# Three weight pieces issued by another engine, and a new order of all steps, in a DeltaNet and MLP kernel

## The chip, the core and the metric

One core of a Trainium2 chip runs the whole program. The metric is device time in microseconds (us), the median of several runs; lower is better. TensorE (PE; PEld are its weight loads) multiplies matrices into PSUM banks, VectorE (DVE), ScalarE (ACT) and GpSimd (POOL) work elementwise, and SyncE (SP) issues DMA transfers. ScalarE and GpSimd issue transfers too. Each engine works off its own list of instructions in order; an instruction that has to wait holds up all that stand behind it on its engine.

## The reference

```python
B, H, S, D = 4, 8, 768, 48
k_n = k / (norm(k) + 1e-6)
for t in range(S):                      # state: D x D for each batch and head
    y[t] = q[t] @ state
    v_old = k_n[t] @ state
    state += beta[t] * outer(k_n[t], v[t] - v_old)
x = y with heads joined                 # B x S x 384
xn = (x - mean) / sqrt(var + 1e-6) * g_ln
out = x + relu(xn @ w_ch1) @ w_ch2      # 384 -> 1536 -> 384
```

The activations are float32. The two weight matrices lie in memory as 64-bit numbers, and the kernel makes float32 of them.

## The kernel before

**Chunks.** The 768 time steps are cut into 12 chunks of 64. Within a chunk the recurrence is written as products: the Gram matrix of the keys, the inverse of a triangular 64x64 matrix for each of the 32 heads, and products with the state that the chunk before left. A head's work is a 64x64 product, so TensorE runs them in groups of 32 or 64 small products.

**The start-up.** Chunk 0 makes its inverse by doubling, in five levels (`first_inverse`). At each level TensorE makes a product with the Gram matrix (L785), VectorE copies the masked part of it (L790), TensorE multiplies the inverse so far by it (L803), and VectorE (L750) and ScalarE (L744) copy the result back for the next level. The bit masks for this are built by VectorE (L465, L471, L477) from two index tables of GpSimd (`xor` and `bits`, L435 and L436). Each level waits for the one before. Then come the queries of chunk 0 (product L837, multiplied by a mask by VectorE, L868), `u` (products L1087, VectorE L1092), the output `y` (L1113, ScalarE copy L1151), its layer norm (VectorE L1157 to L1169, ScalarE L1163), transposes of the normed rows (L1201) and their scaled copies by ScalarE (`xnt`, L1217). At the same time the keys of chunks 2 and 3 are transposed (L635).

Chunk 1's inverse starts from blocks of 16 rows, which VectorE inverts by substitution in a chain of 30 small steps (`rows_inverse`, called x0: L925 and L932). It gets its input from DRAM (`gb`) and writes its result to DRAM (`xd`), from where eight small transfers bring it into place (`xt`). Later pairs of chunks do the same with blocks of 32 rows (x1, x2, ...), and join the blocks by products (L999, L1005).

**The weights.** They come in twelve pieces of two halves, 384 KB each (`fetch`), into five word buffers, three of which are used again. A piece is turned into float32 by four steps (`convert`): ScalarE scales the high words (L599), VectorE shifts them (L604), ScalarE scales the low words (L607), and GpSimd adds both into the weights (L617). Pieces 0 to 5 are `w_ch1`, 6 to 11 `w_ch2`. Pieces 5, 6 and 7 (the sixth to the eighth) go into the buffers that pieces 2, 3 and 4 leave, so their transfers wait for the GpSimd sums of those.

**The MLP.** It follows each chunk (`mlp`). For chunk 0 the first layer is plain products of 128 columns (L1424) with a relu by ScalarE (L1432) and the second is L1466. Chunks 1 and 2 have a first layer in 256 columns (L1444). From chunk 3 on the first layer is made by a scheme of fifteen block products (L1325, with sums by VectorE L1348, ScalarE L1343 and GpSimd L1308), and from chunk 1 on the second layer is made by seven half-size block products (L1541, sums L1528, L1559, L1566). Results go out in `put`.

**The order.** Every piece of work is a step, added by `Line.add` with the engine that does it and the tiles that it reads and writes. The program is not emitted in the order in which the steps are made. A long text, `ORDER`, lists all 3032 step numbers; `Line.emit` walks along it, and `in_this_order` fixes each engine's list to that sequence:

```python
for w in ORDER.split():
    a, b = (0, -1) if w in "fF" else map(int, (w.split("-") * 2)[:2])
    order += self.steps[a : b + 1] or [w]
```

A number may stand anywhere behind the steps that it depends on. An `f` stands for a filler: a product of the identity matrix that nobody reads (`idle`, L1618). The old text has one, in the fifth level of chunk 0's inverse. Waits follow from the tiles alone, so where a step stands decides only what stands before and behind it on its own engine. For transfers that step is the issue: `dma` (L409) issues from the queue of the engine that is named.

Of the kernel before, what the change touches and what calls it, by code (L numbers as in the profile page):

```python
# [159 lines left out]
232 92 97 218 130-131 129 230 220 109 258 253 251 140 137 222 136 91 138 27 31 141 139 142 146 34 143 152 148 24 26 147 158 32 154  # L160
153 231 210 96 145 144 149-151 157 155-156 95 160 159 162 164 161 163 168 28-29 169-170 98 205 165 207 206 174 166 212 167 173 172
171 255 254 252 257 256 395 307 305 176 317 402 405 318 401 47 233 175 178 177 219 184 180 185-186 655 653 658 226 214 182-183 238
188 181 242 187 189 192 259 240 221 209 f 4 179 193 190 194 191 215 223 35 211 250 260-262 241 263 265 201 197 202 204 236 199 203
200 198 309 195 310 264 243 235 234 228 362 237 239 196 329-333 335 353 311 355 312 224 356 361 313-314 354 266-268 337 269-270
338 341 216 315 246 271-288 342-343 289-295 427 321-322 324 323 334 429 336 325-326 347 339-340 348-350 327 344 316 396 399 296
404 406 217 213 328 225 303 298 302 403 301 300 299 468 304 469 426 297 466-467 394 397 400 244 567 569 568 428 345-346 351 571
570 357 572 245 227 352 657 659 229 247 666 660 430 575 593 363 576 359 579-580 594 431 573 583 599 432 407 365 574 584 600 587
577-578 588 358 364 661 410 408 392 409 366 360 605 581 591 368 582 592 606 470 367 411 611 585-586 412 597 589-590 413 598 379
374 612 595-596 603 369 371 601 630 604 602 373 434 1068 668 465 471-474 476-482 414 483-485 667 415 370 372 670 1067 391 669 665
416 609 418 610 420 380 417 631-632 615-617 433 375 419 421-422 633-635 607 618 385 425 386 423-424 435-436 608 381 377 613  # L170
619-620 783 785 782 787 486-498 376 499-507 382 508-511 671-672 378 512 673 383 513 384 1080 916 786 789 788 779 784 918 614 437
440 442 445 441 387 438 443 439 636 621 637 662 638-639 514 444 446-447 450 389 663 674-675 515 388 516 390 1070 1072 677 517 448
790 451 518 449 452 519-539 622-623 457 640 453 641 624-626 1174 780 664 924 676 926 681 540 680 678-679 541 543 542 544 475 642
627 460 456 454 459 458 791 455 794 821-822 825 827 826 831-832 823 828 837 682 824 833 838 843 792 645-647 651 648-650 683-686
848 845 1082 781 1069 688 1071 1073 1084 846 1083 1074 847 1079 545 793 546 834 839 548 550 547 549 551 553 552 555 554 795
689-700 556 829 796 840 830 844 797 835 854 864 917 928 1173 927 925 930 929 923 931 1179 1181 849 922 463 701-705 800 802 798 855
805 706 806 799 1075 856-857 836 865 858 801 841 859 810 842 860 921 1180 643 1183 644 628 1184 629 1185 1365 1171 1178 1182
919-920 932 557 1086 852 862 850 464 851 861 853 866-868 811-812 871 817 1085 461-462 1542 1081 863 803 652 804 933 869 881 872
882 934 807 558 561 819 818 560 559 562 707-710 808-809 711 936 870 712-717 813 883-885 889 886 873-876 878-879 1544 877 887 1087
1554 880 814 816 815 566 564 563 820 565 935 937 972 896-901 890-894 938 973 1546 888 1556 1545 1555 1558 1541 1543 1091 1559  # L180
718-719 1186 978 939 941 720-725 1548 996 726-729 940 895 730 902 731-751 687 1076 979 943 1077 984 974-975 942 907-910 1088 1190
911-912 980 944 946-947 945 913 985 1089 951 981 948 990 976-977 986-987 991 982 1005-1007 983 988 1008-1010 989 994 992 1361 1368
1360 1370 1369 1078 1172 1372 1176 752 904 903 905 1090 997 906 756 753-755 1366 1177 952 949-950 953 955 969 954 1092 956 1093
1367 1371 757-758 1187 768 960 1175 1094 958 1373 1362 1095 957 1374 914-915 959 759 1011 964 999 1002 998 967 1000 968 1547 1003
1012 1022 993 1032 1023-1025 995 1015-1016 1033 1017 760 762 761 763 766 764 767 1188-1189 1549 1191 965-966 1013 1001 1004 1014
765 1018 1026-1027 1019 1034-1036 1020-1021 1192 1040-1041 1037 1042-1045 1375 1030 1557 970-971 1219 1223 1653 1655 1657 1659
1363 1652 1193 1196 769 1194 1842 1648 1654 1656 1658 1840 962 1096 963 1038-1039 1029 1238 1031 1028 1097-1098 1046 1099-1100
2030 1102 1234 1220-1221 773 772 1198 771 1058-1062 1239 1047-1048 1195 1201-1202 770 1197 1199-1200 1203-1204 1103 1560 1224 1376
774 776 775 1206 1049 1063 1050-1052 777 961 778 1227 1553 1377 1064 1207 1104 1053 1105 1205 1106-1110 1208 1111 1101 1112
1235-1236 1228-1229 1237 1230 1251 1231-1232 1252 1210 1233 1240-1241 1209 1253-1254 1378-1379 1246 1242 1247 1222 1243-1244 1270  # L190
1261 1055 1225 1262 1226 1380 1561 1245 2032 1054 1280 1248-1250 1258 1255-1256 1263-1264 1259 1257 1266-1267 1265 1113 1660 1114
1260 1271-1272 1268 1115-1116 1281-1282 1381 1647 1211 1650 1845 1056 1215 1364 1214 1847 1057 1839 1213 1846 1212 1646 1065 1848
1841 1838 1844 1066 2034 1275 1273 1117 1283 1118-1120 1274 1269 1284-1286 1382 1308 1276-1277 1309 1298-1299 1310 1383 1311 1292
1289-1291 1296 1287-1288 1312 1300 1313 1293 1295 1121-1123 1278 1124 1305 1301-1303 1325 1216 1304 1279 1306 1326 1315-1317
1217-1218 1294 1297 1307 1408 2035 1327 1318-1320 1328 1324 1322 2036 1323 1415 2042 1384 1125 1314 1333 1329-1330 1334-1338
1126-1132 1331 1340-1341 1409 1342-1345 1133-1135 1339 1419 2031 1332 1550 1410 1351 1423 1321 1412 1352 1413 1136-1138 1346 1411
1353-1355 1416 1356 1417 1385 1551 1562-1563 1418 2033 1427-1428 1139-1143 1414 1144-1145 1357 1146-1165 1429-1430 1424-1425 1420
1432-1433 1421 1387 1426 1439-1440 1661 1422 1431 1837 1552 1645 1849 1564 1166 1569 1851 1358 1568 1169-1170 1167-1168 1359
# [57 lines left out]
def kernel(  # L256
# [1514 lines left out]
```

## Time and profile before

| What | us |
|---|---|
| Three runs: lowest, median, highest | 513.07, 513.96, 515.15 |
| The profiled execution, its own time | 513.69 |
| Its span | 512.0 |
| TensorE busy | 481.8 (94%) |
| VectorE busy | 357.4 (70%) |
| GpSimd busy | 282.3 (55%) |
| ScalarE busy | 206.2 (40%) |
| TensorE's mean granted clock | 0.983 of full |
| First MLP product (L1424) starts | 60.5 |
| Weight transfers issued by ScalarE (24 of 384 KB) | 12.7 to 91.4 |

A line of the chain of waits says when a stretch of the chain that ended last began, how long it took, and what it was; "issue" is time in which an engine waited for nothing that the profile shows. "ACTq" and "SPq" are the instruction sequencers of ScalarE and SP, here issuing transfers. A line such as "PE by L785 x32" is 32 products of line 785 into the bank `by`.

### The profile page before, as it was taken

The numbers are of one execution on the slowest core, as the hardware profiler recorded it, in microseconds if no ns is written. First come the engines' busy times: TensorE is split into PE (matmuls) and PEld (weight loads), VectorE is DVE, ScalarE is ACT, GpSimd is POOL, SyncE is SP. The second block draws the span as 40 slices with busy tenths as digits, with TensorE's granted clock in tenths as the row PEclk, the third lists the DMA queues.
The fourth block names the chain that finished last, engine by engine and source line by source line (L and its number), as shares of the span: only waits on it lengthen the run. The fifth ranks groups of instructions, "written<-read, shape, count | busy, mean of one in ns | idle before, by whom it ended". The sixth has DMA issues, their size and how long they took to land.

```text
span 512.0 us, 22780 instructions
## 1 busy us (share of the span) xinstructions
PE 481.8 (94%) x9968; PEld 446.6 (87%) x9968; DVE 357.4 (70%) x814; ACT 206.2 (40%) x462; POOL 282.3 (55%) x447
## 2 busy tenths in 40 slices
PE   4677799999999999999999999999999999999997
PEld 3566697768898899899988999999999999999996
DVE  4847658897988667999868898688788436253241
ACT  4577744633443144323334522524513425324130
POOL 8024385224874996784465574634462831654554
PEclk9777999999999999999999999999999999999999
DMA  9986787559456855364644563734424601212011
GB/s 128 257 188 124 211 150 179 123 148 159 82 92 127 204 103 81 85 120 113 136 96 70 105 132 102 130 86 103 88 39 98 140 8 46 52 46 50 2 32 31
DMA packets 181635, 54.56 MB, mean 107 GB/s; under 512 B 164888, under 2 KB 177312, under 8 KB 181536
## 3 DMA queue, kind: packets, MB, share of 16 engines
q1 hardware_dynamic: 168512, 40.10, 38.9%
q10 hardware_dynamic: 10816, 9.83, 6.5%
q0 software_dynamic: 2208, 3.17, 4.0%
q8 instruction: 78, 1.28, 1.1%
q14 instruction: 21, 0.17, 0.1%
HBM read 36.30 MB, written 16.78 MB: 104 GB/s over the span
## 4 chain that ended last, share of the span: by engine, by line
PE 83%; DVE 6%; DMA 3%; issue 3%; SPq 3%; ACT 2%; ACTq 0%; DVEq 0%
PE f L1541 29%; PE f L1325 21%; PE f L1444 6%; PE two L837 3%; PE f L1424 3%; SPq L409 3%; PE by L1051 2%; PE two L1051 2%; PE f L1466 2%; PE two L1106 2%; PE two L1123 2%; PE by L1113 2%; DMA kr<-in_k_dram 2%; PE f L803 1%; PE by L785 1%
## 5 line engine op out<-in xcount | busy, mean ns | idle before, releaser
L1528 POOL TENSOR_TENSOR h_all<-h_all 128x256 f32<-128x256 f32 x99 | 73.5, 755 | 20.4 <-DVE tmp L925 8.4
L1541 PE MATMUL f<-w_sb,h_all 128*128 128x192 f32 x396 | 79.2, 330 | 0.0
L1541 PE MATMUL f<-words,h_all 128*128 128x192 f32 x396 | 77.3, 330 | 0.0
L1348 DVE TENSOR_TENSOR h_all<-f,h_all 128x512 f32<-128x512 f32 x72 | 49.0, 686 | 28.5 <-PE f L1325 21.8
L1541 PEld LDWEIGHTS f<-w_sb,h_all 128*128 128x128 f32 x396 | 65.0, 190 | 1.5 <-issue 0.2
L1541 PEld LDWEIGHTS f<-words,h_all 128*128 128x128 f32 x396 | 64.8, 190 | 0.8
L1566 POOL TENSOR_TENSOR words<-h_all 128x128 f32<-128x128 f32 x66 | 30.0, 472 | 54.0 <-ACT h_all L1352 28.5
L1343 ACT COPY h_all<-f 128x512 f32<-128x512 f32 x45 | 26.2, 585 | 81.3 <-PE f L1325 52.3
L932 DVE TENSOR_TENSOR xb<-xb,tmp 128x31 f32<-128x31 f32 (+19 forms) x139 | 53.6, 386 | 3.5
L925 DVE TENSOR_TENSOR tmp<-xb,gb 128x31 f32<-128x31 f32 (+19 forms) x139 | 51.7, 372 | 4.1 <-POOL xb L912 0.3
L1352 ACT ACTIVATE h_all<-h_all 128x512 f32<-128x512 f32 x54 | 32.5, 626 | 32.5 <-DVE h_all L1348 32.4
L409 POOL DMA_DIRECT2D tb<-in_k_dram x64 | 41.9, 657 | 0.9 <-issue 0.7
L1325 PE MATMUL f<-xnt,w_sb 128*128 128x128 f32 x288 | 39.6, 278 | 0.1
L1325 PE MATMUL f<-x_new,w_sb 128*128 128x128 f32 x288 | 39.5, 277 | 0.0
L1325 PEld LDWEIGHTS f<-x_new,w_sb 128*128 128x128 f32 x288 | 36.4, 192 | 0.3
L1325 PEld LDWEIGHTS f<-xnt,w_sb 128*128 128x128 f32 x288 | 36.0, 192 | 0.6 <-DVE h_all L1348 0.2
L1444 PE MATMUL f<-xnt,w_sb 128*128 128x256 f32 x144 | 33.8, 385 | 0.0
L1559 DVE TENSOR_TENSOR o<-f,x 128x192 f32<-128x192 f32 x33 | 11.3, 348 | 28.4 <-PE f L1541 18.3
L1444 PEld LDWEIGHTS f<-xnt,w_sb 128*128 128x128 f32 x144 | 26.7, 190 | 3.8 <-DVE o L1475 0.4
L1541 PE MATMUL f<-w_sb,words 128*128 128x192 f32 x132 | 26.4, 330 | 0.3 <-DVE o L1559 0.3
L617 POOL TENSOR_TENSOR w_sb<-words 128x768 uint32<-128x768 uint32 (+1 forms) x11 | 14.9, 1365 | 16.4 <-ACT words L607 14.7
L1541 PEld LDWEIGHTS f<-w_sb,words 128*128 128x128 f32 x132 | 21.5, 190 | 0.9 <-DVE o L1559 0.6
(237 smaller groups left out, 976.1 us busy)
## 6 DMA issues: line engine op xcount, KB each, us to landing
words<-in_moe_w_ch_dram ACTq DMA_DIRECT2D x20, 384.0 KB, 4.9
gd<-gsb SPq DMA_DIRECT2D x11, 512.0 KB, 3.7
v<-in_v_dram SPq DMA_DIRECT2D x24, 192.0 KB, 4.1
kr<-in_k_dram SPq DMA_DIRECT2D x46, 96.0 KB, 3.5
out_dram<-o SPq DMA_DIRECT2D x46, 96.0 KB, 2.4
xld<-xlt SPq DMA_DIRECT2D x9, 384.0 KB, 2.3
xnt<-xld SPq DMA_DIRECT2D x36, 96.0 KB, 2.9
tb<-in_q_dram SPq DMA_DIRECT2D x40, 64.0 KB, 3.7
```

The lines of the kernel that those rows point to most:

```text
L409: add(eng, cost, lambda: QUEUE[eng].dma_start(out=out_, in_=in_), r, w, bulk=n * ns / 16e3, np=n, **kw)
L925: lambda j=j, n=n, w=w, t=t: nc.vector.tensor_tensor(out=t, in0=xv[:, 0:n, j : j + 1].to_broadcast([128, n, w]), in1=gv[:, j : j + 1, j + ...
L932: "DVE", dve(n * w), lambda t=t, rest=rest: nc.vector.tensor_tensor(out=rest, in0=rest, in1=t, op=ALU.subtract),
L1051: nc.tensor.matmul(dst[half(e), hp, j], src[drows(hp), (e if n else key_half(c, hp, e)) * GP + j], s_all[drows(hp), e, j], start=(n == 0 o ...
L1325: nc.tensor.matmul(wide(p[:, f : f + 128]), w[:, f : f + 128], r, start=start and i == 0, stop=True, skip_group_check=True)
L1343: add("ACT", act(512), lambda: nc.scalar.copy(o, p), pk, ok)
L1348: add("DVE", dve(512), lambda: nc.vector.tensor_tensor(out=o, in0=x, in1=y, op=op), [*xk_, *yk], ok)
L1352: add("ACT", act(512), lambda: nc.scalar.activation(o, o, ACTF.Relu, scale=scale), [], ok)
L1444: nc.tensor.matmul(p[:, 0:TOK], w1_sb[:, t, f * 128 : (f + 1) * 128], xnt[:, t], start=(t == 0), stop=(t == KC - 1))
L1528: add(eng, cost, lambda: e.tensor_tensor(out=out_, in0=x, in1=y, op=op), r, w, port=2 if eng == "Pool" else 1, pr=-2)
L1541: lambda f=f, t=start and f == order[0]: nc.tensor.matmul(p[:, 0:D2], lhs(f), rhs[:, f], start=t, stop=(f == order[-1]), skip_group_check=True
L1566: lambda f=f + i: e.tensor_tensor(out=s3[f], in0=one(0, 0)[0](f), in1=one(1, 0)[0](f), op=ALU.subtract),
```

## The change

The diff has two parts. In `fetch`, the six transfers of the sixth to the eighth piece are issued by SP in place of ScalarE:

```diff
         for a in range(2):
             dma(
-                "ACT", dst[:, a], src[:, a].rearrange("p (b x) -> p b x", x=2 * RUN), 384, 54,
+                "SP" if 5 <= i < 8 else "ACT", dst[:, a], src[:, a].rearrange("p (b x) -> p b x", x=2 * RUN), 384, 54,
                 w=[("wd", BUF[i], a)], after=after, **kw,
             )
```

The other part is a new text `ORDER`, 96 lines in place of 95, of which the first three are shown:

```diff
 ORDER = """
-51-52 54 58 53 55 57 319 56 63 62 306 398 67 308 393 66 320 7 65 64 9 8 59 61 60 249 11 10 48 12 49 654 656 50 248 68 0 3 2 13
-71-72 46 40 44-45 42-43 41 101-102 1 75 36 82-84 76-77 73-74 37 103 38 104 99 93 39 94 100 90 85-86 78 15 14 69 208 87 89 105-108
-16-18 79-80 70 81 110 88 111 114-118 121 119 113 120 124 112 122 25 19-20 125 123 132 126 134 6 5 22 133 30 128 127 33 21 23 135
+52 54 0 2 53 58 51 57 56 55 319 63 66 306 394 308 62 67 320 64 249 7-8 48 9 65 60 10 49 59 11-12 14 16 21-22 18 6 13 3 72 71 42 61
+654 656 248 68 101-102 40 46 43 50 44 41 45 1 75 82 76 83 73 77 84 36 74 104 103 37-38 100 99 93 39 94 105-106 34 24 33 19 78
+85-86 79 69 23 107 89 87 80 20 15 70 88 81 17 116-117 110 118 111-112 122 90 121 120 113 108 119 124-125 132 123 31 208 114-115
...
```

The steps are the same in number and kind, but for the filler, which is gone. What each engine's list becomes, by the place of each step in it (the six moved transfers left out):

| Engine | Steps | In the same place | Within three places | Over ten places off | Farthest |
|---|---|---|---|---|---|
| TensorE | 954 | 201 | 646 | 32 | 25 |
| VectorE | 814 | 152 | 596 | 64 | 89 |
| ScalarE | 483 | 103 | 385 | 9 | 41 |
| GpSimd | 443 | 66 | 315 | 32 | 70 |
| SP | 332 | 40 | 171 | 65 | 65 |

On SP the moved transfers stand as follows among the first steps of its list: the sixth piece's first half behind the loads of chunk 3's keys, then the seventh's second half, a `beta_b` load, the second half of chunk 1's queries, the sixth's second half, a load for chunk 1's norms, the seventh's first half, four more small loads, the write of chunk 2's Gram matrix, the eighth's second half, a `beta_b` load, the write of x0's result, and the eighth's first half. At the end of chunk 0's inverse TensorE's list was: level-5 product (one half of the heads), filler, level-5 product (the other half), half of the queries, both last products of the inverse, transposes of chunk 2's keys, the other half of the queries. It is now: both level-5 products, one of the last products, both halves of the queries, `u` for half of the heads, the other last product.

More of the change, by code (lines that the diff above doesn't have):

```diff
@@ L161 @@
[L161 to L188, printed above, removed]
@@ L252 @@
+2957-2958 2897-2898 2888-2889 2961 2959 2926 2960 2970-2971 2980-2981 2972-2973 2982-2985 2974-2975 2986 2964 2962-2963 2967 2977
+2968 3005-3006 2976 2965-2966 2969 2978 2987 2950 2997-2998 3007-3008 2988 2979 2951 3009 2999-3002 2989 3010 3003 3012-3013 2990
+3014 2991-2992 3015-3017 3011 3018 2993-2996 3004 3023-3028 3019-3020 3029 3021 3030 3022 3031
 """
```

154 lines of the change are left out of this document (90 added, 64 removed).

## The prediction

> **What bounds the kernel now.** I read the 40 slices first, then the busy times of three long stretches, then the chain of waits of the first 70 us, then the clock.
>
> ```profile
> PE   4677799999999999999999999999999999999997
> ...
> PEclk9777999999999999999999999999999999999999
> DMA  9986787559456855364644563734424601212011
> ```
>
> TensorE is under 80% busy in the first five slices (64 us) and full from there to the last one. The clock is below full in slices 2 to 4, and the DMA engines are busiest in the first eight.
>
> ```profile
> 0.00:63.00 63.00, 40.67 (x1231) 35.11 (x1232) 39.85 (x130) 41.59 (x97) 24.79 (x43) 0.86 0.84 178
> 63.00:504.00 441.00, 436.91 (x8716) 407.77 (x8716) 316.25 (x681) 164.61 (x366) 255.73 (x402) 1.00 0.46 97
> 504.00:512.00 8.00, 4.20 (x25) 3.67 (x23) 1.34 (x4) 0.00 (x0) 1.74 (x3) 0.96 0.18 49
> ```
>
> Columns: stretch, its length, busy us of PE, PEld, DVE, ACT, POOL, granted clock, DMA share, GB/s. TensorE idles 63 - 40.67 = 22.3 us before 63 us and 441 - 436.91 = 4.1 us in the 441 us after it. The matrix work is the same in both kernels but for one filler product, so the change can gain a few us in the start-up, at most 4 in the long stretch, and can lose in both.
>
> ```profile
> 39.98 1.13 PE by L785 x32
> 41.11 0.72 PE two L1618 x2
> 41.84 1.30 PE two L785 x32
> 43.14 0.76 PE by L837 x27
> 43.90 0.98 PE f L803 x51
> ...
> 45.31 0.37 ACTq L409
> ...
> 45.73 0.50 ACTq L409
> ...
> 46.91 0.65 PE f L635 x4
> ...
> 50.79 0.84 issue
> ...
> 56.75 1.10 issue
> ```
>
> This is the chain (start, us, what) where chunk 0's inverse ends. The reader should see a filler on it (L1618), two weight issues of ScalarE (ACTq L409) between copies that TensorE waits for, and TensorE standing for "issue" in the middle of groups of products, while DMA is heavy.
>
> **The change, part by part.** All times are those of the profiled execution. T is the start of VectorE's mask multiply of chunk 0's queries (L868), at 46.82; the MLP's first product (L1424) starts at 60.53, 13.7 us after T.
>
> *Before T, at the inverse's end.* From 39.98 to T the old TensorE order is: level-5 product 1.13, filler 0.72, level-5 product 1.30, half of the queries 0.76, both last products of the inverse (L803) 0.98, transposes of chunk 2's keys (L635) 0.65, the other half of the queries 0.50 + 0.32 wait + 0.46; with hops, 6.84. In the new one the filler is gone (-0.72), one of the two L803 groups (half of 0.98, -0.5) and the key transposes (-0.65) stand behind the second half of the queries. Sum -1.87. The second level-5 product has its input: its VectorE copy ended at 40.51, so the filler's time is free to be saved. Bounds: 0 (something else ends last) and -2.2 (its 0.32 wait goes too).
>
> *Before T, in VectorE's queue.* Mask building that stands between dependent steps at 18.61 (0.26 and 0.30) and 21.88 (two memsets of 0.27) moves to the front, where VectorE idles from 3.18 to 6.31 waiting for GpSimd's `bits`; GpSimd now makes `bits` ahead of two of its DMA issues (0.65 and 0.80). One mask step of 0.2 comes in between instead: -0.9. Against it, ScalarE's two square roots of the key norms (9.03 and 9.49) now stand behind the copy of the first keys, some 0.4 later, while chunk 1's keys are issued one place (0.65) sooner. I take 0 for these two together, bounds -0.7 and +0.7.
>
> *The moved issues.* Six issues of 0.55 leave ScalarE (3.3 us of its queue between 45.31 and 51.78; 0.87 is on the chain above). On SP each needs its word buffer free: the sixth piece's first half goes at about 38, but the seventh's waits for GpSimd's sum of the fourth piece (L617, 48.22 to 49.68 now, some 2 us sooner in the new order), and SP stands there. Behind it: one `beta_b` load, half of chunk 1's queries, the sixth piece's second half, the norm loads, the write of chunk 2's Gram matrix. Chunk 1's queries would land at about 52, their transposes stand at 54.98 and 59.79 now: hidden, by 3 us or more. The eighth piece's last half to go stands behind the write of x0's result (L409 xd, which waits for the L925/L932 chain, over at 57.81).
>
> *From T to the first MLP product.* VectorE in the new order: mask multiply 1.22, first `u` 0.56, one weight shift (L604) 0.56, the L925/L932 chain with the layer norm's steps 8.41 (49.40 to 57.81), second `u` 0.55: 11.3. Then either shift 0.42 and GpSimd's weight sum 0.82, or transposes of the normed rows 0.55 and three scaled copies 0.89: 12.5 to 12.9 against 13.7. I take -0.8; bounds 0 and -1.2. So the first MLP product comes 1.87 + 0.9 + 0.8 = 3.6 us sooner, near 57.
>
> *What is late next.* The fifth feature block needs the sum of a second weight half (L617); counted the same way it is ready at T + 17.4, and the old order uses it at 64.58, T + 17.8: of the 0.8 only 0.4 stays (+0.4). The eighth piece's last half is issued at about T + 12 and lands 4.9 later (median of its group), T + 16.9; ScalarE wants it at T + 15.5, with the MLP's relus queued behind. Three banks of products cover most of that 1.4: +0.3, bounds 0 and +1.4.
>
> *The long stretch.* Of 954 TensorE steps 646 stay within three places, the largest move is 25. Loads of `k` by GpSimd move up to 25 places and SP's up to 41 in the first 150 us. Counting TensorE work between each load and its user in both orders, 62 users stand short of the median landing in the old order and 59 in the new. I take 0; bounds -2 (half of the 4.1 us idle) and +4 (twice that idle).
>
> Sum: -3.6 + 0.4 + 0.3 = -2.9. The profiled execution took 513.69 (span 512.0, 1.7 around it), 0.27 under the median of the runs, 513.96. Taken from the median: 511.1.
>
> **The clock.**
>
> ```profile
> 19.78:26.60 6.82, 5.91 (x160) 5.30 (x164) 4.59 (x18) 4.34 (x10) 0.00 (x0) 0.50 0.91 293
> 26.60:33.43 6.83, 4.31 (x181) 3.61 (x178) 4.01 (x14) 5.02 (x16) 0.00 (x0) 1.00 0.90 235
> 33.43:40.26 6.83, 4.78 (x153) 4.21 (x147) 3.69 (x11) 4.92 (x12) 5.33 (x7) 0.50 0.88 117
> 40.26:43.67 3.41, 3.41 (x97) 3.00 (x97) 1.19 (x4) 2.88 (x7) 0.22 (x1) 0.50 0.48 59
> ```
>
> The granted clock goes back to full after stretches with 5.91 of 6.82 and 3.41 of 3.41 us busy, and to half after one with 4.31 of 6.83. The removed filler lies in the last of these, and gives 0.72 of its 3.41. Without it the next product follows at once, so I forecast the same clock. The Trainium skill (TensorE: Matmul & The Clock Gate, "HAM oscillation — how this bites in real kernels") has the half clock come back after an idle gap of more than about 3.4 us. This trace differs: it fell to half after a stretch whose longest stand is 1.38 us. By the page a missing filler could not matter; by the trace it could.
>
> **The rivals.**
>
> *Given back.* The start-up shortens, but waits for weights and loads behind SP's stand take its place in the first MLP block. For it: SP stands some 9 us, and TensorE already waits for L617 at 60.53 (0.34). Against it: the 3 us of cover. The gain falls to about 0.5: 513.4.
>
> *Half clock.* One mechanism: the stretches near 27 and 41 us fall under what the gate wants, and the start-up runs at half until the MLP. A 32-product group (L785) takes 0.69 at full (18.07) and 1.13 at half (39.98), 1.64 times. The chain has 3.1 us of TensorE work from 26.6 to 33.4 and 10.2 from 43.7 to 60; 13.3 x 0.64 = 8.5 if all counts, and I take 5.5, since VectorE's 11.3 us chain covers part. 513.96 - 2.9 + 5.5 = 516.6. It decides from the point where the extra passes 2.9 us, that is 4.5 us of chain work at half. For it: two of five stretches were that thin. Against it: a shorter chain is a denser one.
>
> *Waits in the long stretch.* The new places cost TensorE four or five further waits of about 1 us, like the 1.1 of the chain at 56.75, over eleven chunks: 511.1 + 4 = 515.1 and up. For it: 308 TensorE steps moved by over three places. Against it: the count of short users is no larger.
>
> *Stalls go too.* The "issue" stands of 1.38, 1.00, 0.84 and 1.10 us (29.72, 35.77, 50.79, 56.75) all fall where transfers are dense; with transfers spread out, three of the four (3.3) go: 507.8. For it: none as long stands elsewhere before 200 us. Against it: pieces one to five stay where they were.
>
> *Not what it says.* The pieces go when their buffers come free, as now; then only ScalarE's 0.87 is saved. That would be 513.1, and is counted with the second case.
>
> **How the numbers follow.** Shorter start-up, kept: 0.48, own range 509.2 to 512.9. Given back: 0.16. Half clock: 0.13. Waits in the long stretch: 0.11. Stalls go: 0.12. The predicted time is the first's, 511.1. The range goes from the stalls' case, 507.8, to just under the half clock's, 516.4. No change means within 0.5% (2.6 us), what runs of this kernel can tell. Faster (under 511.4): 0.29 of the first case and 0.11 of the stalls' case, 0.40. Slower (over 516.5): 0.10 of the half clock, 0.10 of the long stretch, 0.03 of the second: 0.23. Within: 0.37.
>
> **What would show it.** Right: no L1618 rows; L868 near 44 and the first L1424 near 57; ScalarE's chain without ACTq L409 after 31; TensorE's idle time before 63 us near 19. Wrong: half clock after the first L868; TensorE waiting at L1424 for L617, or ScalarE at L599 for a `words` load; idle time in the 441 us clearly over 4.1.

## The result, and the profile after

| Kernel | Median us | Lowest to highest | Executions | Ratio to the old kernel, 95% interval |
|---|---|---|---|---|
| before | 513.31 | 509.39 to 515.83 | 22 | |
| after | 515.54 | 512.35 to 519.26 | 22 | 1.0051 [1.0033, 1.0069] |

The changed kernel is 0.5% slower. Its profiled execution took 513.22 us (span 511.5), the second fastest of the 22, so its trace shows less than the whole loss. The executions differ by their mean granted clock: the ten at 0.983, like the profiled one, took 514.4 us on average, the seven at 0.976 or 0.977 took 516.3, the three at 0.970 took 517.6. A second profile of the same kernel (a_again below, 515.83 us, clock 0.977) is nearer to the middle, and both are read here. In the new file each line number is higher by one: the old L868 is L869.

The 40 slices of the changed kernel:

```profile
PE   4477899999998999999999999999999999999996
...
PEclk9688999999999999999999999999999999999999
DMA  9877786687525865542863616723525501121001
```

TensorE is emptier in slice 2 and fuller in slice 5, and a digit 8 has come in the long stretch, in slice 13 (153 to 166 us). The three long stretches again (columns as in the prediction):

```profile
0.00:63.00 63.00, 41.74 (x1298) 35.52 (x1299) 40.86 (x131) 42.79 (x99) 25.49 (x43) 0.86 0.82 181
63.00:504.00 441.00, 436.29 (x8649) 406.46 (x8649) 316.61 (x680) 164.23 (x364) 252.44 (x401) 1.00 0.46 97
504.00:511.50 7.50, 3.65 (x23) 3.35 (x21) 0.98 (x3) 0.00 (x0) 3.06 (x5) 1.00 0.19 52
```

Idle time before 63 us fell from 22.3 to 21.3, in the long stretch it rose from 4.1 to 4.7. The chain where the first MLP product is made ready:

```profile
44.21 1.16 issue
47.50 1.02 PE f L636 x4
48.52 1.04 PE by L1088 x32
49.55 1.04 PE f L636 x4
50.59 0.83 PE by L1114 x32
```

The filler and ScalarE's weight issues are gone from it. In their place come an "issue" stand in the middle of the product of the first `u` (L1088), and products and transposes at half clock. Just before, at the end of chunk 0's inverse, the clock is full where the old profile has half (33.43 to 43.67 us, in the prediction):

```profile
30.58:47.65 17.07, 11.70 (x525) 9.69 (x518) 12.41 (x37) 14.54 (x37) 8.39 (x11) 1.00 0.70 174
```

Where time comes and goes is seen best from step to step. This table is worked out from the traces. It takes the TensorE steps that the old kernel starts at 130.5, 196.5 and 507.2 us, and gives the start of the step with the same place in each kernel's list, less the old kernel's.

| Kernel | at 130.5 us | at 196.5 us | at 507.2 us |
|---|---|---|---|
| after | -1.98 | -0.62 | -0.55 |
| a_again (the same kernel) | -1.53 | +2.02 | +2.02 |
| h_rest | +1.31 | +4.52 | +4.68 |
| h_start | -0.26 | -0.47 | -0.23 |
| a_both | -0.85 | +0.35 | +1.03 |
| a_port | +0.16 | -0.14 | +0.39 |
| a_pf | -2.34 | -2.43 | -2.22 |

The changed kernel is ahead by 1.5 to 2.0 us at about 129 us and loses 1.4 to 3.6 us up to 196 us. Behind that it wins and loses nothing.

### The profile page after: what moved, and what is told of

Read it like the earlier page. It is cut to its first block, busy times and chain, and to the rows that moved or that the text cites. A ratio compares the mean times of both kernels' runs of the same rounds, so it can differ in the third digit from the quotient of the medians.

```text
span 511.5 us, 22778 instructions
## 1 busy us (share of the span) xinstructions
PE 481.7 (94%) x9966; PEld 445.3 (87%) x9966; DVE 358.5 (70%) x814; ACT 207.0 (40%) x462; POOL 281.0 (55%) x447
## 3 DMA queue, kind: packets, MB, share of 16 engines
q8 instruction: 78, 1.28, 1.0%
## 4 chain that ended last, share of the span: by engine, by line
PE 79%; DVE 4%; ACT 4%; issue 2%; SPq 1%; DMA 1%; ACTq 1%; POOL 0%; DVEq 0%
PE f L1542 29%; PE f L1326 21%; PE f L1445 6%; PE two L838 4%; PE f L1467 3%; PE by L1052 2%; PE two L1052 2%; PE by L1114 2%; PE two L1107 2%; SPq L410 1%; PE two L1124 1%; PE f L1425 1%; DVE h_all L1349 1%; ACT xt L745 1%; PE by L1006 1%
## 5 line engine op out<-in xcount | busy, mean ns | idle before, releaser
L1542 PE MATMUL f<-w_sb,h_all 128*128 128x192 f32 x396 | 81.5, 330 | 0.0
L1567 POOL TENSOR_TENSOR words<-h_all 128x128 f32<-128x128 f32 x66 | 29.6, 467 | 49.3 <-ACT h_all L1353 22.3
L933 DVE TENSOR_TENSOR xb<-xb,tmp 128x31 f32<-128x31 f32 (+19 forms) x139 | 51.7, 372 | 3.6
L1326 PE MATMUL f<-xnt,w_sb 128*128 128x128 f32 x288 | 40.8, 277 | 0.3 <-DVE h_all L1349 0.3
L690 POOL TENSOR_TENSOR v<-v,kpair 128x768 f32<-128x768 f32 x10 | 14.8, 1478 | 17.1 <-DVE pt L916 16.4
```

Of the source, the lines that this page charges most:

```text
L933: "DVE", dve(n * w), lambda t=t, rest=rest: nc.vector.tensor_tensor(out=rest, in0=rest, in1=t, op=ALU.subtract),
L1326: nc.tensor.matmul(wide(p[:, f : f + 128]), w[:, f : f + 128], r, start=start and i == 0, stop=True, skip_group_check=True)
L1542: lambda f=f, t=start and f == order[0]: nc.tensor.matmul(p[:, 0:D2], lhs(f), rhs[:, f], start=t, stop=(f == order[-1]), skip_group_check=True
L1567: lambda f=f + i: e.tensor_tensor(out=s3[f], in0=one(0, 0)[0](f), in1=one(1, 0)[0](f), op=ALU.subtract),
```

## The experiments

All edits are to the text `ORDER` (numbers are steps), but for the first two, which also or only touch the queue of the three pieces. No step is left out. Each ratio is to the old kernel, run beside it on the same chip.

**Which part of the change loses.** Four kernels take the change apart. q_only has the old order and the new queue; o_only the new order and the old queue:

```diff
-                "SP" if 5 <= i < 8 else "ACT", dst[:, a], src[:, a].rearrange("p (b x) -> p b x", x=2 * RUN), 384, 54,
+                "ACT", dst[:, a], src[:, a].rearrange("p (b x) -> p b x", x=2 * RUN), 384, 54,
```

> The order of before, with the sixth to eighth weight piece issued by SP (each transfer at its old place in the order). If the queue is what costs (SP stands at a piece whose buffer is not free, and loads wait behind it), the time is 0.3 to 0.6% over before's, as the changed kernel's is (ratio 1.0051). If the new order is what costs, the ratio is 0.998 to 1.001: six issues of 0.55 us leave ScalarE, of which at most 0.87 us was on the chain.

Measured: 513.96 us, 0.9992 [0.9972, 1.0013]. The queue alone changes nothing that these runs can tell.

> The new order, with all weight pieces issued by ScalarE as before. If the order costs, the ratio to before stays at 1.003 to 1.007; if the queue costs, it falls to 0.997 to 1.001.

Measured: 524.63 us, 1.0215 [1.0185, 1.0244]. The waits for TensorE of this kernel, between 63 and 126 us (who waited, for whom, us in total, times, longest):

```profile
PE f L1425 <- ACT h_all L1433: 5.9, 4, 4.7
```

With the issues back in ScalarE's list, its relus stand behind scaling steps that wait 3.24 and 1.14 us for weight transfers (69.66 and 71.67 us). The new order cannot do without the new queue, so the parts do not simply add.

h_start has the new order and queue up to the first MLP product, then the old order; h_rest the old order and queue up to there, then the new order:

```diff
-... 427 429 428 213 569 226 570 355 393 397 ...
+... 427 429 428 213 393 405 655 226 362 355 ...
```

> The new order and SP's queue up to the first MLP product, and from there all remaining steps in the order of before. If the start-up costs (more of it at half clock: in the 22 runs of the changed kernel those at a mean clock of 0.983 took 514.4 us in the mean, those at 0.977 took 516.3 and those at 0.970 took 517.6), the ratio is 1.003 to 1.007 and the mean clock is often 0.977 or less. If the long stretch costs, the ratio is 0.996 to 1.000, since the profile of the changed kernel had 1.1 us less idle time before 63 us.

Measured: 514.05 us, 0.9992 [0.9966, 1.0018]. It is 1.98 us ahead near 61 us and gives nearly all of it back at once: stands of 1.28 us (71.5) and 1.27 (81.7) that the changed kernel doesn't have.

```diff
-... 397 400 244 567 569 568 428 345-346 ...
+... 397 400 244 428 569-570 567 783 665 345-346 ...
```

> The order of before up to the first MLP product, and from there the remaining steps in the new order, all pieces issued by ScalarE. If the start-up costs, the ratio is 0.998 to 1.002; if the long stretch costs (waits of 1 us and more on TensorE, such as the 1.54 us at 155.6 in the profile of the changed kernel), it is 1.003 to 1.007.

Measured: 517.88 us, 1.0076 [1.0053, 1.01]. The loss is in the later order: 3.2 us of it between 130 and 196 us (the table).

**Where it loses.** In the changed kernel's TensorE row near 155 us (start, us, engine, line, what, count, and in brackets the idle time before and what ended it):

```profile
153.97 0.94 PE L1124 MATMUL two<-u,kr 64*48 64x48 f32 x64
154.72 0.86 PE L1114 MATMUL by<-u,pt 64*64 64x48 f32 x43
157.12 0.50 PE L1114 MATMUL by<-u,pt 64*64 64x48 f32 x19 [1.54 <-issue]
157.41 0.27 PE L838 MATMUL two<-kt 48*64 48x64 f32 x2
157.46 0.23 PE L1114 MATMUL by<-u,pt 64*64 64x48 f32 x2
157.48 1.15 PE L838 MATMUL two<-kt 48*64 48x64 f32 x62
```

TensorE stops in the middle of 64 equal products whose inputs are all there. Every kernel with the changed kernel's order at this place stops ahead of the same record. The list of DMA queues has one for instructions:

```profile
q8 instruction: 78, 1.28, 1.0%
```

78 packets of 16 KB go with some 20,000 records of TensorE (products and weight loads, PE and PEld), that is one for 256. I numbered TensorE's records by start, from 0, the records of its sequencer included (137 in the changed kernel), in all 19 traces of this case. Of the stands of 0.5 us or more, 56 are called "issue" by the profile, and all 56 come ahead of a record whose number leaves 193 when divided by 256 (7,105 here); of the 194 with a named cause none does. So these stands are the ends of blocks of instructions. In this case the packet for the next block began at 154.69, ended at 155.57, and TensorE went on at 157.12. All 56 stands ended 1.2 to 1.7 us behind the end of a packet (1.4 in the middle), and it was always the packet whose number fits: 27 had ended ahead of record 7,105, which is 193 + 27 x 256. The old kernel's four "issue" stands in the prediction (29.72, 35.77, 50.79, 56.75) come ahead of records 961, 1217, 1985 and 2241, which are block ends too.

The Trainium skill (Runtime: NRT & Kernel Launch, "Instruction fetch mechanics") has the refill in 16 KiB blocks of 256 instructions and calls crossing a block mostly hidden. The blocks agree with the trace; hidden it is not here, where 64 small products and their weight loads are 128 records in 0.94 us, so that a block of them lasts about 2 us, while a packet takes 0.88 us or more and TensorE goes on 1.4 us behind it.

Four kernels test this. a_again is the changed kernel as it is.

> The changed kernel once more, unaltered, as the yardstick for the three others. Two theories of its 2 us loss. Refill: TensorE's instruction stream comes in blocks of 256, a packet of 16 KB each; where the packet for the next block goes out late, TensorE stands in the middle of a group of small products; the new order has such a stand of 1.54 us in y of chunk 3 (155.6 us) which the old one has not. Clock: the new start-up spends more 3.41 us stretches at half clock, in most executions more than in the profiled one (clock 0.983). Both expect a median of 515 to 516; refill expects the stand again at the same instruction, the 7,105th record of TensorE and its weight loads, 1.5 to 2.4 us long; clock expects a mean clock of 0.977 to 0.980.

Measured: 516.76 us, 1.0048 [1.0021, 1.0074]; a stand of 2.09 us at the 7,105th record; mean clock 0.977. Its trace shows what a longer stand does next (stretches behind the stand's start; columns as before, the clock is the one after the engines):

```profile
156.04:159.50 3.46, 1.37 (x85) 1.36 (x85) 3.32 (x9) 0.71 (x2) 1.97 (x4) 1.00 0.58 104
159.50:162.90 3.40, 3.40 (x18) 3.09 (x10) 1.65 (x5) 1.16 (x2) 0.00 (x0) 0.50 0.40 151
162.90:166.30 3.40, 3.40 (x135) 3.02 (x134) 2.00 (x8) 1.46 (x3) 0.00 (x0) 1.00 0.14 18
```

A stretch with TensorE busy 1.37 of 3.46 us is followed by 3.4 us at half clock, in the middle of the long stretch. In the traces this came behind stands of 1.53 (b_hold, near 84 us), 1.86 (h_rest), 2.09 (here and in a_swap), 2.17, 2.37 and 2.43 us, not behind 1.23, 1.54 or 1.72, nor behind the 2.09 of a_chain. It is one reason why the executions spread by their clock: this trace has 6.8 us more of half clock than the one shown first, 3.4 here and 3.4 in the start-up.

a_ahead moves three MLP products ahead of `s`:

```diff
-... 973 938-939 941 940 1076 909 942 910-911 978 ...
+... 973 938 909-911 939 941 940 1076 942 978 ...
```

> The changed kernel with three MLP products of one step each (feature block 3 of the second chunk's MLP) put ahead of s of chunk 3 where they stood behind G6. Same work, and s, y and G6 stand 12 records later in TensorE's stream. Refill: the packet is asked for some 40 records into a block; s now begins 54 records into it, not 42, so the packet goes out while the three products run, some 1 us sooner: the stand falls to under 0.5 us, and the time by 1.0 to 1.5 us against the unaltered kernel of the same job. Clock, or a real wait of y for its data: no change in the median (within 0.3), a stand of 1 us or more near 156.

Measured: 514.87 us, 1.001 [0.9986, 1.0034]; stand 1.23 us, not under 0.5. The direction was right, and the median is 1.9 us under a_again's; what holds the packet was not. Its trace still loses 1.3 us between 130 and 196 us, as the changed kernel's fast profiled execution does, but no half clock follows the stand.

h_127 keeps the changed kernel to its 126th TensorE step and then goes on with the old order:

```diff
-... 650 698-703 651 704 796 927 925 644 930 ...
+... 650 698-703 651 704 1067 918 848 1069 1084 ...
```

> The changed kernel's order, queue included, up to its 126th TensorE step (127 us), then the old order's rest. Refill: in the profiles the new order is 2.1 us ahead at 127 us and loses 1.8 of it by 190; with the old rest the lead stays, and the median is 1.5 to 2 us under the unaltered changed kernel's, 513.5 to 514, at or under the old kernel's. Clock: the start-up is the same as in the changed kernel and so is the loss, 515 to 516.

Measured: 516.18 us, 1.0027 [0.9994, 1.006]: missed. No stand at 7,105, but a wait that neither parent has, and half clock behind it:

```profile
PE f L1541 <- POOL h_all L1528: 2.4, 1, 2.4
```

Two good halves of an order need not fit at the seam.

a_fill puts fillers where TensorE waits 5.4 us for the inverse's first product:

```diff
-... 110 118 111-112 122 ...
+... 110 118 111-112 F F F 122 ...
```

> The changed kernel with three filler products of 512 columns ahead of the inverse's first step, where TensorE stands 5.4 us (12.78 to 18.17) and the clock falls to half for 13.65 us behind it. Clock: full clock from 17 to 30 us; some 10 us of TensorE work there at half becomes 6, VectorE's and ScalarE's parts of the chain stay, so first MLP product 2 to 3 us sooner than 59.2, and the median 2 to 3 us under the unaltered one. Refill: the fillers add 12 records ahead of s of chunk 3 as well, so the stand near 156 goes (1.0 to 1.5 us), and nothing else changes; the first MLP product comes within 0.5 us of 59.2. If the stand behind the fillers only turns the clock's fall to a later stretch, first MLP product near 59 and the clock's mean as in the unaltered kernel.

Measured: 516.62 us, 1.0039 [1.0008, 1.007]. The clock stays full to 45.5 us and the mask multiply comes 2 us sooner (41.12), but then 13.7 us of half clock follow and the first MLP product comes at 60.63. The stand at 7,105 stayed (2.17), with `s` 12 records later: the distance of `s` from the block's start does not decide. The mean clock rose to 0.983 and the time did not fall. As the fillers only moved the half clock to a later part of the start-up, this run does not tell what that clock costs; that the loss lies behind the start-up is shown by h_start and h_rest.

**What makes the packet late.** In the changed kernel the packet goes 4.7 us behind the block's first record; in the old kernel, in q_only and in h_start 0.7 to 1.1 us. Two waits stand in between: `s` for `u` of chunk 3 (ScalarE, behind a relu), and product 907 for VectorE's sum 895. a_swap takes the first away, a_both both, a_ahead4 leaves both and gives more time:

```diff
-... 973 938-939 ...
+... 938 973 939 ...
```

> The changed kernel with two steps of ScalarE swapped: the copy of u of chunk 3 ahead of the relu h of the third chunk's MLP, as the old order has it (its input is there at 147.8, but behind the relu it goes at 151.6). Two waits could hold TensorE's reading ahead, and with it the packet for the next 256 instructions: s of chunk 3 for u (152.35), or the product 907 (feature block 3) for VectorE's sum 895 (152.68). Held by u: the packet goes 3 us sooner, no stand near 156, median 2 to 3 us under the unaltered changed kernel (516 in the jobs so far), 513 to 514. Held by 907: the stand stays, 1.5 to 2.4 us, and the median 515.5 to 516.5.

Measured: 515.84 us, 1.0034 [1.0004, 1.0065]; stand 2.09 us. Not `u`.

```diff
-... 907-908 901 721-727 973 938-939 941 940 1076 909 942 ...
+... 901 721-727 938 973 939 941 940 1076 907-909 942 ...
```

> The changed kernel with both waits taken out of the way: u ahead of the relu, and the products 907 and 908 behind G6, next to 909 to 911, so that they follow VectorE's sum by 3 us. Refill, with either hold: packet before 152, no stand at the 7,105th record, no half clock behind it, and the median 2 to 3 us under the unaltered changed kernel's 516: 513 to 514, ratio to the old kernel 0.996 to 0.999. If the stand is set by the three dense groups alone, s, y and G6 one behind the other, it stays at 1 us or more and the median at 515.5 to 516.5.

Measured: 516.16 us, 1.0038 [1.0015, 1.006]. The packet goes 0.89 us behind the block's first record and the stand at 7,105 is gone, as expected; the time is not. TensorE's only wait between 125 and 205 us is now the product G6 behind it, for VectorE's `s_all`:

```profile
PE two L838 <- DVE s_all L1134: 1.7, 1, 1.7
```

```diff
-... 973 938-939 941 940 1076 909 942 910-911 978 ...
+... 973 938 909-911 978 939 941 940 1076 942 ...
```

> The changed kernel with four MLP products ahead of s of chunk 3: 909 to 911 as in the run with three, and the m2 product 978 of 1.4 us. Neither hold is touched; s, y and G6 come 2.4 us later behind the packet instead of 1.0. Refill: packet 2.0 to 2.5 us behind VectorE's sum 895, TensorE able to go on 2.5 us behind the packet's start, so at about 157.4 against a boundary reached at 158.0: stand under 0.3 us, no half clock, median 513 to 514. Dense groups alone: stand of 1 us or more, median 515 to 516.5.

Measured: 515.81 us, 1.0035 [1.0009, 1.006]. No stand at 7,105; waits of 0.6 to 1.0 us at four other places up to 203 us, two for ScalarE (0.61 and 0.64), one for VectorE (0.71) and one for GpSimd (1.03). So to take the stand away is not enough: something else is late. In a_both it is VectorE; a_ahead4 doesn't tell.

b_hold gives the old order the wait of `s` for `u` and an earlier `s`:

```diff
-... 938 973 1546 888 ... 1186 978 939 941 720-725 ...
+... 973 938 1546 888 ... 1186 939 941 978 720-725 ...
```

> The other way round: the old kernel, all of its order and queue, with two steps put as the new order has them: the copy of u of chunk 3 behind the relu (u ready near 153 instead of 151.1), and the m2 product 978 behind y, so that s starts 1.4 us sooner, near 155.0. Work and transfers are the same. Refill, held by u: packet near 155.2, ready near 157.8, boundary reached near 156.3: a stand of 1.0 to 1.6 us at the 7,105th record, followed in some executions by 3.4 us or more of half clock, and the median 1 to 3 us over the old kernel's. If the new order's other moves make the stand, or the 907 hold alone: no stand there, and the old kernel's time within 0.5 us.

Measured: 514.15 us, 0.9994 [0.9965, 1.0023], no stand. The packet began at 155.15, ahead of the end of `u` (155.49): again not `u`. But `s` came only at 157.84, so the wait that this run was to make did not arise, and it says less than a_swap.

**What makes VectorE late.** The changed kernel's VectorE and GpSimd ahead of the sum 895 (the row at 152.33):

```profile
148.11 2.38 DVE L926 TENSOR_TENSOR tmp<-qt,pt 128x255 f32<-128x255 f32 x1
148.24 1.41 POOL L1529 TENSOR_TENSOR h_all<-h_all 128x256 f32<-128x256 f32 x2
149.61 0.59 POOL L1560 TENSOR_TENSOR o<-o,x 128x192 f32<-128x192 f32 x1
150.52 0.42 DVE L933 TENSOR_TENSOR qt<-qt,tmp 128x255 f32<-128x255 f32 x1
150.86 1.24 DVE L817 STREAM_TRANSPOSE qt<-tb 128x1024 f32<-128x1024 f32 x1
152.03 0.38 DVE L926 TENSOR_TENSOR tmp<-qt,pt 128x256 f32<-128x256 f32 x1
152.33 0.35 DVE L1560 TENSOR_TENSOR o<-f,x 128x192 f32<-128x192 f32 x1
```

The same multiply in the old kernel:

```profile
149.73 0.38 DVE L925 TENSOR_TENSOR tmp<-qt,pt 128x255 f32<-128x255 f32 x1
```

Step 718 takes 2.38 us in place of 0.38. It begins as GpSimd begins three steps (879, 878, 888) one behind the other, and ends 0.3 us after the last of them. It took 2.37 or 2.38 us in all ten traces with the new order at this place, and 0.38 in all five with the old one. Over all 19 traces, the scan's steps on 250 to 256 columns that met no such GpSimd step (`TENSOR_TENSOR`) took 0.37 to 0.44 us, 585 of 585; all 223 that took over 0.6 met one. The old order has its own long meeting, at 227.49 us (2.29), and TensorE waits 0.3 us there, so a meeting need not cost TensorE its own length. The Trainium skill (SBUF — State Buffer, "Who interferes with whom") says that a `tensor_tensor` of VectorE with both inputs in SBUF contends with GpSimd's reads, one blocking until the other is done. The trace agrees, and shows one VectorE step wait out three GpSimd steps.

a_port takes that meeting away: 718 and 719 behind the transposes 1186, 720 behind the sum 895, 888 behind seven load issues, and `u` ahead of the relu:

```diff
-... 879 878 888 464 461 1556 1545 1555 1546 1543 1547 1558 462 718-719 1186 720 ...
+... 879 878 464 461 1556 1545 1555 1546 1543 1547 1558 888 462 1186 718-719 ...
-... 896-897 895 898-900 907-908 901 721-727 973 938-939 ...
+... 896-897 895 720 898-900 907-908 901 721-727 938 973 939 ...
```

> The changed kernel with four moves near 150 us and nothing else: VectorE's 718 and 719 (scan of chunk 4) behind the transposes 1186, 720 behind the sum 895, GpSimd's 888 behind its next seven load issues, u of chunk 3 ahead of the relu. Port theory: in the new order VectorE's 718 stands 2.38 us (0.42 elsewhere) until GpSimd's 879, 878 and 888 are over, and 895, s_all and the packet of instructions are all late by that. Here 718 meets only the end of 878: 718 under 1.2 us, 895 near 151 instead of 152.7, packet before 152, no stand at the 7,105th record and none over 0.5 us at G6, no half clock near 160, loss between 126 and 196 us under 0.5 us, and a median of 513 to 514.3 against 515.8 to 516.7 for the changed kernel and its relatives. Rival, the new places of products and loads in general: another wait of 1 us or more appears between 126 and 200 us and the median stays at 515.5 or more.

Measured: 513.47 us, 0.9987 [0.9958, 1.0015]. VectorE and TensorE in this kernel:

```profile
151.41 0.69 DVE L926 TENSOR_TENSOR tmp<-qt,pt 128x255 f32<-128x255 f32 x1
...
152.47 0.35 DVE L1560 TENSOR_TENSOR o<-f,x 128x192 f32<-128x192 f32 x1
...
155.86 0.94 PE L1124 MATMUL two<-u,kr 64*48 64x48 f32 x64
156.62 1.21 PE L1114 MATMUL by<-u,pt 64*64 64x48 f32 x64
157.94 1.16 PE L838 MATMUL two<-kt 48*64 48x64 f32 x64
```

The multiply takes 0.69. (This execution reached the table's first step 1.7 us later than a_again, so the times in the expectation that count from the start came later too.) The sum begins 3.4 us ahead of `s` (1.6 in the changed kernel); the multiply itself gives 1.7 of that, and 720, now behind the sum, 0.3. The 64 products of `y` run through, no half clock follows, and nothing is lost between 130 and 196 us (the table). The three later kernels with these moves have the multiply at 0.68 or 0.69 and no stand at the 7,105th record either. The four moves were not tried singly but for `u`, which alone had no effect. And a_ahead, which leaves the meeting as it is, comes close in time: its interval (0.9986 to 1.0034) overlaps that of a_port, and only the traces set the two apart.

**Where the start-up's gain goes.** The mask multiply comes at 43.06, 3.8 us sooner than before, the first MLP product at 59.20, 1.3 sooner. Between them VectorE waits 1.49 us for the first `u`, 1.10 for the layer norm and 1.00 for the second `u`, with its scan (x0) in line behind. a_chain moves parts of the scan ahead of these:

```diff
-... 196 329-330 356 395 401 235 406 241 ... 243 217 266 337 267 312 331 309 311 332 334 ... 325 353 268-281 ...
+... 196 266-271 329-330 356 395 401 235 406 241 ... 243 217 272-275 337 312 331 309 311 276-279 332 334 ... 325 353 280-281 ...
```

> The changed kernel with ten steps of VectorE's scan of chunk 0 moved up in its own queue: six ahead of the first u, four ahead of the layer norm's first statistics, four ahead of the second u, where VectorE stands 1.49, 1.10 and 1.00 us for TensorE and ScalarE. Queue theory: the first MLP product follows the mask multiply by 16.1 to 17.4 us, not 13.7 as in the old kernel, because VectorE's scan waits in line behind those three; with the waits filled the scan ends 2.5 to 3.3 us sooner and the first MLP product comes near 57 (59.2 to 61 without). The loss at 156 us stays, so the median falls by 1 to 3 us against the changed kernel, 513 to 515. Rival, the weights: the words of the first weights bound the first MLP product, it stays within 0.7 us of 59.2 to 61, and the median stays at 515.5 to 516.7.

Measured: 517.73 us, 1.0061 [1.003, 1.0092]: missed. The scan is sooner, but then VectorE waits at the layer norm's last part for ScalarE, which has that square root behind the copies of transposes that TensorE makes, here at half clock for 13.7 us:

```profile
DVE rstd L1167 <- ACT rstd L1164: 4.2, 1, 4.2
```

The first MLP product comes at 63.57. a_pc has both:

> Both of the above. If the start-up's waits and the meeting on the port are the whole loss, the gains add up: median 511 to 513, under the old kernel (ratio 0.994 to 0.998). If only one of the theories holds, it is as that run alone; if TensorE's clock takes the start-up's gain, a mean clock of 0.977 or less and a median of 514 or more.

Measured: 515.01 us, 1.0 [0.9971, 1.003]. By the medians a_chain's moves make a_port 1.5 us slower; the intervals overlap.

What the new start-ups have in common is a stand at the 1,729th record, in the product of the first `u` (0.32 us ahead of that record before, in a product of the queries). With one exception, the longer it is, the later the first MLP product comes behind the mask multiply, in the nine traces whose start-up is not edited otherwise: stands of 0.70 (h_start), 1.16, 1.44 (three), 1.71, 1.99, 2.54 and 2.81 us go with 14.3, 16.1, 16.5 to 17.5, 17.6, 18.0, 18.3 and 17.6 us. The half clock behind the stand goes along: none with 14.3, 3.4 us with 16.1, 16.5 and the last 17.6, and 6.8 with the other five. The old order had transposes of 0.65 us each, of 8 records, among these small products; the new one has four groups without a break. a_pf is a_port with a filler there, a_pff has the three of a_fill as well:

```diff
-... 264 196 329-330 356 ...
+... 264 196 F 329-330 356 ...
```

> The kernel of the run without the meeting near 150 us, and one filler product of 512 columns (4 records, 1.46 us at full clock) ahead of the product of the first u, where TensorE stands 2.54 us at the 1,729th record and is busy 0.81 of 3.41 us. Clock theory: TensorE busy over 2 us in that stretch, no half clock from 47 to 54 us; products and transposes behind it (1.0 us each at half) take 0.65; the stand shrinks by about the filler's length; the first MLP product comes 1 to 2 us sooner than 61.5, the mean clock rises to 0.981 or more and the median falls by 0.5 to 1.5 us under 513.5. If the stand alone is what costs, the filler only fills it: half clock gone, first MLP product within 0.7 us of 61, median 513 to 514. If the filler pushes u's product later by its own length, first MLP product 62 or later.

Measured: 511.81 us, 0.9959 [0.9939, 0.998]: faster than both kernels. The stretches in a_port, then in a_pf:

```profile
43.50:46.90 3.40, 0.81 (x28) 0.56 (x31) 0.86 (x1) 1.85 (x3) 0.74 (x2) 0.99 0.52 145
46.90:50.30 3.40, 3.00 (x77) 2.72 (x76) 1.46 (x4) 1.97 (x5) 1.47 (x1) 0.50 0.94 200
```

```profile
44.00:47.41 3.41, 1.96 (x73) 1.32 (x73) 1.44 (x3) 1.73 (x3) 1.33 (x2) 1.00 0.57 171
47.41:50.82 3.41, 2.86 (x84) 2.15 (x85) 2.03 (x8) 2.85 (x7) 2.29 (x2) 1.00 0.89 209
```

In the stretch that holds the stand TensorE is busy 1.96 of 3.41 us in place of 0.81 of 3.40, and the clock behind stays full. The stand is 1.28 us (2.54 in a_port), the first MLP product comes at 59.79 (61.48), and the mean clock of the executions is 0.985 (0.978). The stand's own length varies from trace to trace, so how much of the gain is the clock and how much a sooner packet isn't separated. Nor do the times alone show that the filler gains over a_port: the two intervals overlap.

> The same and three fillers of 512 columns ahead of the inverse's first product (TensorE stands there 4.5 us, near 13 us). With the three fillers alone the changed kernel had full clock to 45 us and the mask multiply 2 us sooner (41.1), but half clock from 45.5 to 59.2. Clock theory: with both stands filled, full clock throughout, mask multiply near 41, first MLP product 57 to 58.5, mean clock 0.99, median 510.5 to 512.5 and faster than the old kernel by 0.4 to 0.8%. If the half clock only moves on to a later stretch: first MLP product 60 or later, median 513 or more.

Measured: 511.68 us, 0.9959 [0.9933, 0.9984], as fast, but not by the way that was expected: the fillers push the inverse's first product back, the mask multiply comes at 44.59, the first MLP product at 60.23, and 10.2 us of half clock remain in the start-up.

## Why the prediction was wrong

It gave 511.1 us, a gain, with no change or slower against it; measured were 515.54, a loss. Two steps failed: the long stretch, taken as 0, which lost 1.4 to 3.6 us, and the way from T to the first MLP product, taken as -0.8, which was 2.4 us longer. Term by term:

*Before T, both terms* (-1.87 and -0.9): right by their sign, and in part by luck. The mask multiply L869 came at 43.06, 3.76 us sooner, where "near 44" was forecast. Up to the level-5 product it was 1.38 us sooner, from there to T another 2.38. But the forecast took the clock as unchanged, and at the inverse's end it was full in place of half: the first level-5 group of 32 products took 0.69 us, not 1.13. In h_start, with the same steps and half clock from 38.13 to 44.96, the multiply came at 44.21, 2.6 us sooner, close to the 2.8 of the two terms. So the order's own part may well be about that and the rest the clock's; why the clock was full there no run shows.

*The moved issues*, hidden: right (q_only 0.9992). That the new order needs them moved (o_only 1.0215) was not said.

*From T to the first MLP product* (-0.8): wrong by its sign. It took 16.1 us in the profile, and 14.3 to 18.3 in other traces with that start-up and no edit between, against 13.7. The step added up VectorE's own work (its terms give 12.5 to 12.7, not 12.9) and took TensorE's part as ready. In the trace VectorE waits 3.6 us there: 1.49 for TensorE, which stands for instructions, 1.10 for ScalarE's copy of `y`, and 1.00 for the product of the second `u`, which comes behind a group of transposes at half clock (48.52, in the chain). So the first MLP product came 1.3 us sooner, not 3.6.

*What is late next*: not seen. TensorE's only wait of over 0.3 us between 63 and 120 us is 0.37, and the lead does not shrink there but grows, from 1.3 to 2.0 us.

*The long stretch*, taken as 0 with bounds of -2 and +4: this step decided the sign. It lost 1.4 us in the fast profiled execution and 3.6 in a_again. The step counted loads against their users, and the loads were not late. What was late was one VectorE multiply, 2 us longer where it met three GpSimd steps; behind it the sum that frees a bank, the product that waits for it, the packet of instructions, and in some traces the clock. The a_port kernel undoes this and is level with the old one.

The rivals. *Waits in the long stretch* came nearest: 515.1 and up was the time. Its mechanism, four or five waits of 1 us over eleven chunks, was not it: it was one place. *Given back* and *Half clock* were each partly so: the gain of the start-up shrank from 3.8 to 1.3 us, by a stand and by half clock behind it, but not at SP's stand nor through thin work before 44 us. *Stalls go too* had the cause wrong: the stands come where block ends fall into dense groups; that traffic of the DMA engines delays the packets was not tested. After the first L869 the clock did fall to half (47.65 us), the sign that was named for *Half clock*.

The clock paragraph said that a stretch with too little TensorE work brings half clock, even with no long stand. That held, but not as a sharp line. In the 19 traces, between 10 and 505 us and in stretches of 3.41 us counted from the clock's changes, all 48 falls to half came behind a stretch with TensorE busy 1.88 us or less, and none behind 1.91 or more. But five stretches with 1.44 to 1.84 were not followed by a fall, two of them in the old kernel (12.95 and 53.91). Full clock came back behind 2.89 us or more; 14 stretches with 2.95 to 3.41 were followed by more half clock.

What stays open: what exactly releases the packet of the next block. Over all blocks it goes 0.85 to 1.19 us behind the start of the block before the one that it brings (the median, by trace), and 1.9 to 2.8 us behind the end of the sum 895 where product 907 waits for it. The runs show that `u` is not the one that holds it. a_both differs from a_swap by the place of 907 and 908 alone, and there the packet goes 0.9 in place of 5.2 us behind the block's first record, so the place of 907, with its wait, decides there; by what rule stays open. What a_both wins by the packet it loses again at G6, which waits 1.72 us for VectorE.

## What to carry to other kernels

An order of steps that is checked against lengths of steps and dependencies says nothing of two things that showed here: VectorE and GpSimd steps with inputs in SBUF that meet (2.0 us for one multiply), and long runs of small products at the end of a block of 256 TensorE instructions (stands of 0.5 to 2.9 us). Where the profile says "issue", count TensorE's records: if the number leaves the same remainder by 256 each time, it is the instruction stream, and work of few, long instructions ahead of the dense group can shorten the stand, a filler if need be (2.54 to 1.28 us in a_pf). When a stand is taken away and the time stays, look for the engine that is late behind it before looking for the next stand.

## What was not expected of the hardware

All 56 of TensorE's unexplained stands of 0.5 us or more in 19 traces come at ends of 256-record blocks, and last up to 2.9 us. One VectorE multiply of 0.38 us waited out three GpSimd steps in a row (2.38). Behind a stand of 1.5 to 2.4 us in a stretch that is otherwise full, TensorE ran 3.4 to 6.8 us at half clock in seven traces, and in three it did not (1.54, 1.72 and 2.09).
